# A windowed-attention and highway-layer kernel: the last sum and the doubling of x on GpSimd, with another order of the loads

## The chip, the cores and the metric

The kernel runs on one core of a Trainium2 chip. The metric is the device time in microseconds (us) of one execution. A core has five engines that run their own instruction streams and wait for each other through semaphores: TensorE (PE, matmuls), VectorE (DVE), ScalarE (ACT), GpSimd (POOL) and SyncE (SP). Here POOL issues all loads and SP issues the bias load and all stores.

## What is computed

The inputs are float32: q, k and v of shape (4, 8, 768, 64), that is 4 batches, 8 heads, 768 positions, 64 values per head; two 512 x 512 weights and a bias of 512. The output is (3072, 512) float32. In short:

```python
scores = (q @ k.T) / sqrt(64)            # per batch and head
keep = (pos_k < 4) | ((0 <= pos_q - pos_k) & (pos_q - pos_k < 128))
a = softmax(where(keep, scores, -1e9))
x = (a @ v) with the heads side by side  # (3072, 512)
H = relu(x @ w_h)
T = sigmoid(x @ w_t + b_t)
out = T * H + (1 - T) * x
```

A position sees the 128 positions up to itself and the first 4 positions of its batch (the sinks). The second half is a highway layer on the attention output.

## The kernel before, in words

The 3072 rows are cut into 24 blocks of 128 rows, 6 per batch; a block's window lies in itself and the block before it. All matmul operands are float16, which the loads cast to. Beside each head's 64 columns of v stands a column of 2.0, so that the row sum comes out doubled and the scaled result, xh, is half of x. With u = tanh of half the gate's input and hps = xh @ w_h, the output is 2·xh + (u + 1)·(max(hps, 0) - xh).

One loop (L335 to L357) runs over i from -2 to 24 and is a software pipeline written out by hand: in iteration i, block i+1 has its scores made (stage_S), block i its attention output (stage_A), block i+2 its transposes (stage_T), block i-1 its highway layer (stage_Mt, stage_Mh). The order of PE, DVE and ACT instructions is as written there.

- stage_T (L178): PE transposes q and k of a block (L182, L184), ACT copies the one (qT, L187), DVE the other (kT, L188).
- stage_S (L228): score matmuls (L242), and ACT takes the exponent into e (L245), in two halves. stage_sink (L214): the scores of the sinks, sk (L222), and their exponent es (L225), for two blocks at a time.
- stage_mask (L251): DVE multiplies each half of e by a 0/1 mask (L258).
- stage_A (L262): PE multiplies by v (L273, L279); DVE takes the reciprocal of the row sums (rec, L286) and scales (xh, L288).
- stage_X (L293): PE transposes xh (L297), ACT copies it to xT (L299).
- stage_sink_setup (L191), once per batch: DVE copies L198, PE vps (L203), DVE vs (L207).
- stage_Mt (L304): gate matmuls into tps (L307, L309), ACT tanh into u (L312).
- stage_Mh (L315): matmuls into hps (L321); then three DVE instructions: dd = max(hps, 0) - xh (L324), ee = (u + 1)·dd (L327), otok = 2·xh + ee (L330); SP stores otok (L332).

Loads: load(n) issues two DMAs from POOL (q, L84; k, L85), load_v(n) one (v, L92). The loads of blocks 0 to 7 (AHEAD = 8) are put out before the loop in a list written by hand (L106 to L138), with the weights w_t (L122) after the q and k of block 2 and w_h (L125) after the q and k of block 3. In the loop, loads run 8 blocks ahead of stage_T (L345 to L347). Buffers: 8 for q and for k (sd_pool), a ring of 11 for v (v_ring), 4 for xh (x_pool), 3 each for u, dd and ee (td_pool), 4 for otok (o_pool). A POOL DMA also waits until the POOL DMA eight places before it has landed. POOL's instructions in the loop are ordered by the framework's scheduler, which each kernel's build fixes.

Before the loop DVE fills the v buffers with 2.0 (L104, one memset each) and makes the masks' variants (L140 to L145).

Of the kernel before, what the change touches and what calls it, by code (L numbers as in the profile page):

```python
# [9 lines left out]
FP16 = mybir.dt.float16  # L10
FP32 = mybir.dt.float32
AF = mybir.ActivationFunctionType
ALU = mybir.AluOpType
ENG = mybir.EngineType
# [7 lines left out]
def kernel(  # L22
# [18 lines left out]
    nc = tc.nc  # L41
    P = 128

    B, H, S, D = q.shape
    NSINK = int(n_sink)
# [4 lines left out]
    NT, DM = out.shape  # L50
# [4 lines left out]
    NB = NT // P  # L55
    NHP = H // 2
    NOC = DM // P
    SCALE = 1.0 / math.sqrt(D)
    VW = H * 65 + 64
    AHEAD = 8  # L60

    const = ctx.enter_context(tc.tile_pool(name="const", bufs=1))
    sd_pool = ctx.enter_context(tc.tile_pool(name="p_sd", bufs=AHEAD))
    qkT_pool = ctx.enter_context(tc.tile_pool(name="p_qkT", bufs=5))
    e_pool = ctx.enter_context(tc.tile_pool(name="p_e", bufs=5))
    es_pool = ctx.enter_context(tc.tile_pool(name="p_es", bufs=2))
# [2 lines left out]
    td_pool = ctx.enter_context(tc.tile_pool(name="p_td", bufs=3))  # L69
# [2 lines left out]
    av_ps = ctx.enter_context(tc.tile_pool(name="ps_av", bufs=1, space=bass.MemoryType.PSUM))  # L72
    m_ps = ctx.enter_context(tc.tile_pool(name="ps_m", bufs=2, space=bass.MemoryType.PSUM))

    NV = AHEAD + 3
    v_ring = [const.tile([P, VW], FP16, tag=f"v{i}", name=f"v{i}") for i in range(NV)]
    qk_sd = {}

    def load(n):
        b, c = divmod(n, NSC)  # L80
        rows = slice(c * P, (c + 1) * P)
        qsd = sd_pool.tile([P, H, D], FP16, tag="qsd", name="qsd")
        ksd = sd_pool.tile([P, H, D], FP16, tag="ksd", name="ksd")
        nc.gpsimd.dma_start(out=qsd, in_=q[b, :, rows, :].transpose([1, 0, 2]))  # L84
        nc.gpsimd.dma_start(out=ksd, in_=k[b, :, rows, :].transpose([1, 0, 2]))  # L85
        qk_sd[n] = (qsd, ksd)

    def load_v(n):
        b, c = divmod(n, NSC)
        rows = slice(c * P, (c + 1) * P)  # L90
        vt = v_ring[n % NV][:, 0:H * 65].rearrange("p (h e) -> p h e", e=65)
        nc.gpsimd.dma_start(out=vt[:, :, 0:D], in_=v[b, :, rows, :].transpose([1, 0, 2]))  # L92
# [1 line left out]

    ebias = const.tile([P, 1], FP32, tag="ebias")
    nc.vector.memset(ebias, _EXP_BIAS)
    wh_sb = const.tile([P, NOC, DM], FP16, tag="wh")
    wt_sb = const.tile([P, NOC, DM], FP16, tag="wt")
    ident = const.tile([P, P], FP16, tag="ident")
    mask = const.tile([P, 2, P], FP16, tag="mask", name="mask")  # L100
    nc.vector.memset(ident, 1.0)
    nc.vector.memset(mask, 1.0)
    for vt in v_ring:
        nc.vector.memset(vt, 2.0)  # L104

    with tc.manual_schedule(engines={ENG.Pool}):  # L106
        load(0)
        nc.gpsimd.affine_select(
            out=ident, in_=ident, compare_op=ALU.is_equal, fill=0.0,
            base=0, pattern=[[-1, P]], channel_multiplier=1)  # L110
        load_v(0)
        load(1)

        nc.gpsimd.affine_select(
            out=mask[:, 1, :], in_=mask[:, 1, :], compare_op=ALU.is_ge, fill=0.0,
            base=0, pattern=[[1, P]], channel_multiplier=-1)
        load_v(1)
        nc.gpsimd.affine_select(
            out=mask[:, 0, :], in_=mask[:, 0, :], compare_op=ALU.is_ge, fill=0.0,
            base=-1, pattern=[[-1, P]], channel_multiplier=1)  # L120
        load(2)
        nc.gpsimd.dma_start(out=wt_sb, in_=moe_w_t.rearrange("(kc p) of -> p kc of", p=P))  # L122
        load_v(2)
        load(3)
        nc.gpsimd.dma_start(out=wh_sb, in_=moe_w_h.rearrange("(kc p) of -> p kc of", p=P))  # L125
        load_v(3)
        bdm = const.tile([P, H], FP32, tag="bdm")
        nc.gpsimd.memset(bdm, 1.0)
        bdm3 = bdm.rearrange("p (a b) -> p a b", b=2)
        nc.gpsimd.affine_select(  # L130
            out=bdm3, in_=bdm3, compare_op=ALU.is_ge, fill=0.0,
            base=0, pattern=[[-32, NHP], [-4, 2]], channel_multiplier=1)
        nc.gpsimd.affine_select(
            out=bdm3, in_=bdm3, compare_op=ALU.is_ge, fill=0.0,
            base=NSINK - 1, pattern=[[32, NHP], [4, 2]], channel_multiplier=-1)
        for n in range(4, AHEAD):
            load(n)
            load_v(n)  # L138

    mask0 = const.tile([P, P], FP16, tag="mask0", name="mask0")  # L140
    nc.vector.tensor_copy(out=mask0, in_=mask[:, 1, :])
    nc.vector.memset(mask0[0:NSINK, :], 1.0)
    mask1 = const.tile([P, 2, P], FP16, tag="mask1", name="mask1")
    nc.vector.tensor_copy(out=mask1, in_=mask)
    nc.vector.memset(mask1[0:NSINK, 0, :], 1.0)  # L145


    bt32 = const.tile([1, DM], FP32, tag="bt32")
# [11 lines left out]
    for hh in range(2):  # L160
        nc.vector.tensor_copy(
            out=sel[:, :, 4 * hh:4 * hh + NSINK],
            in_=ident[:, 0:NSINK].unsqueeze(1).to_broadcast([P, NHP, NSINK]))
    ks_bd = []
    for i in range(2):
        t = const.tile([P, NHP * 160], FP16, tag=f"ks{i}", name=f"ks{i}")
# [24 lines left out]
    def stage_sink_setup(b):  # L191
# [8 lines left out]
        vps = av_ps.tile([P, 2, 512], FP32, tag="av", name="vps")  # L200
        vt = v_ring[(b * NSC) % NV]
        for g in range(2):
# [11 lines left out]
    def stage_sink(n):  # L214

        b = n // NSC
        ks = ks_bd[b % 2]
        sk = m_ps.tile([P, 2, P], FP32, tag="m", name="sk")
        for t in range(2):
            qT, _ = qkT[n + t]  # L220
            for hp in range(NHP):
                nc.tensor.matmul(sk[:, t, :], lhsT=ks[:, hp * P:(hp + 1) * P],  # L222
                                 rhs=qT[:, hp, :], start=(hp == 0), stop=(hp == NHP - 1))
        es = es_pool.tile([P, 2, P], FP16, tag="es", name="es")
        nc.scalar.activation(out=es, in_=sk, func=AF.Exp, bias=ebias, scale=SCALE)  # L225
        es_of[n] = es_of[n + 1] = es
# [35 lines left out]
    def stage_A(n):  # L262
        b, c = divmod(n, NSC)
        es, np_ = e_of.pop(n)
        vts = ([] if c == 0 else [v_ring[(n - 1) % NV]]) + [v_ring[n % NV]]
        av = av_ps.tile([P, 2, 4, P], FP32, tag="av", name="av")
# [33 lines left out]
        xT_of[n] = xT  # L300

    u_of = {}

    def stage_Mt(n):  # L304
        xT = xT_of[n]
        tps = m_ps.tile([P, DM], FP32, tag="m", name="tps")
        nc.tensor.matmul(tps, lhsT=ones_row, rhs=bt16, start=True, stop=False)  # L307
        for kc in range(NOC):
            nc.tensor.matmul(tps, lhsT=xT[:, kc, :], rhs=wt_sb[:, kc, :],  # L309
                             start=False, stop=(kc == NOC - 1))  # L310
        u = td_pool.tile([P, DM], FP16, tag="u", name="u")
        nc.scalar.activation(out=u, in_=tps, func=AF.Tanh)  # L312
        u_of[n] = u

    def stage_Mh(n):  # L315
        xT = xT_of.pop(n)
        xh = xh_of.pop(n).rearrange("p h d -> p (h d)")
        u = u_of.pop(n)
        hps = m_ps.tile([P, DM], FP32, tag="m", name="hps")
        for kc in range(NOC):  # L320
            nc.tensor.matmul(hps, lhsT=xT[:, kc, :], rhs=wh_sb[:, kc, :],  # L321
                             start=(kc == 0), stop=(kc == NOC - 1))
        dd = td_pool.tile([P, DM], FP16, tag="dd", name="dd")
        nc.vector.scalar_tensor_tensor(out=dd, in0=hps, scalar=0.0, in1=xh,  # L324
                                       op0=ALU.max, op1=ALU.subtract)
        ee = td_pool.tile([P, DM], FP16, tag="ee", name="ee")
        nc.vector.scalar_tensor_tensor(out=ee, in0=u, scalar=1.0, in1=dd,  # L327
                                       op0=ALU.add, op1=ALU.mult)
        otok = o_pool.tile([P, DM], FP32, tag="otok", name="otok")
        nc.vector.scalar_tensor_tensor(out=otok, in0=xh, scalar=2.0, in1=ee,  # L330
                                       op0=ALU.mult, op1=ALU.add)
        nc.sync.dma_start(out=out[n * P:(n + 1) * P, :], in_=otok)  # L332

    with tc.manual_schedule(engines={ENG.PE, ENG.DVE, ENG.Activation}):
        for i in range(-2, NB + 1):  # L335
            s = i + 1
            if 0 <= i < NB and i % NSC >= 2 and i % 2 == 0:
                stage_sink(i)
            if 0 <= s < NB:
                stage_S(s)  # L340
            if 0 <= i < NB:
                stage_A(i)
            if i + 2 < NB:
                stage_T(i + 2)
            if i + 2 + AHEAD < NB:  # L345
                load(i + 2 + AHEAD)
                load_v(i + 2 + AHEAD)  # L347
            if 0 <= s < NB:
                stage_mask(s)
            if 0 <= i - 1 < NB:  # L350
                stage_Mt(i - 1)
            if 0 <= i < NB:
                stage_X(i)
            if 0 <= i < NB and i % NSC == 0:
                stage_sink_setup(i // NSC)
            if 0 <= i - 1 < NB:
                stage_Mh(i - 1)  # L357
# [35 lines left out]
```

The softmax here doesn't subtract the row's maximum and nothing guards it: scores larger than these inputs give would overflow.

## Time and profile before

| | |
|---|---|
| median of 3 runs | 140.11 us (139.75 to 140.7) |
| the profiled execution, its own time | 140.7 us |
| its span, first to last instruction | 139.0 us |
| its TensorE clock, granted | 0.993 |
| ACT busy | 90.4 us (65% of the span) |
| POOL busy | 66.2 us (48%), all of it before 87.5 us |
| mean of one load issue on POOL | 0.89 us |
| store of one block, issue to landing (median) | 2.9 us |

Busy times are sums over an engine's instructions; matmuls are pipelined and their ends are modelled, so PE's busy time is not time at its peak. An idle time before an instruction is put down to the semaphore that came last. The chain of waits is followed back from the last instruction; it names the work that each microsecond of the span was spent on.

### The profile page before, as it was taken

The numbers are of one execution on the slowest core, as the hardware profiler recorded it, in microseconds if no ns is written. First come the engines' busy times: TensorE is split into PE (matmuls) and PEld (weight loads), VectorE is DVE, ScalarE is ACT, GpSimd is POOL, SyncE is SP. The second block draws the span as 40 slices with busy tenths as digits, with TensorE's granted clock in tenths as the row PEclk, the third lists the DMA queues.
The fourth block names the chain that finished last, engine by engine and source line by source line (L and its number), as shares of the span: only waits on it lengthen the run. The fifth ranks groups of instructions, "written<-read, shape, count | busy, mean of one in ns | idle before, by whom it ended". The sixth has DMA issues, their size and how long they took to land.

```text
span 139.0 us, 3303 instructions
## 1 busy us (share of the span) xinstructions
PE 114.6 (82%) x1312; PEld 74.1 (53%) x1312; DVE 117.2 (84%) x235; ACT 90.4 (65%) x129; POOL 66.2 (48%) x84
## 2 busy tenths in 40 slices
PE   0306879999999699999999699999996999999730
PEld 0105656756764465667565457657652665675300
DVE  6895466689988999899898999898989998999590
ACT  3015961879775957987777497779767777873310
POOL 6999785899887987876758170000000000000000
PEclk9999999999999999999999999999999999999997
DMA  1999999999999999999999959221011021101111
GB/s 9 113 127 120 158 189 162 152 171 178 203 191 168 200 200 174 181 201 185 185 159 144 186 72 134 80 78 75 5 75 75 0 80 75 70 11 75 75 75 75
DMA packets 79408, 16.98 MB, mean 122 GB/s; under 512 B 75297, under 2 KB 76321, under 8 KB 79394
## 3 DMA queue, kind: packets, MB, share of 16 engines
q0 software_dynamic: 75936, 10.49, 112.2%
q1 hardware_dynamic: 3458, 6.30, 12.4%
q8 instruction: 10, 0.16, 0.5%
q14 instruction: 4, 0.03, 0.1%
HBM read 20.97 MB, written 6.29 MB: 196 GB/s over the span
## 4 chain that ended last, share of the span: by engine, by line
DVE 42%; PE 33%; ACT 14%; issue 8%; DVEq 0%
PE hps L321 12%; ACT e L245 9%; DVE ee L327 6%; DVE otok L330 6%; DVE e L258 6%; DVE dd L324 6%; DVE xh L288 5%; PE av L273 4%; PE tps L309 4%; DVE kT L188 4%; PE xtp L297 3%; ACT qT L187 3%; PE sps L242 3%; PE sk L222 3%; DVE vs L207 2%
## 5 line engine op out<-in xcount | busy, mean ns | idle before, releaser
L245 ACT ACTIVATE e<-sps,ebias 128x1024 f16<-128x1024 f32 (+1 forms) x48 | 47.4, 1039 | 17.5 <-PE sps L242 13.3
L309 PE MATMUL tps<-wt_sb,xT 128*128 128x512 f16 x96 | 25.5, 390 | 0.0
L321 PE MATMUL hps<-wh_sb,xT 128*128 128x512 f16 x96 | 24.6, 378 | 0.7
L84 POOL DMA_DIRECT2D qsd<-in_q_dram x24 | 21.5, 895 | 5.3 <-DMA wt_sb<-in_moe_w_t_dram 1.2
L85 POOL DMA_DIRECT2D ksd<-in_k_dram x24 | 21.4, 890 | 2.3 <-DMA wh_sb<-in_moe_w_h_dram 1.2
L273 PEld LDWEIGHTS <-e 128*128 128x128 f16 x352 | 20.4, 100 | 3.9 <-DVE vs L207 0.9
L312 ACT ACTIVATE u<-tps 128x512 f16<-128x512 f32 x24 | 14.4, 600 | 9.5 <-PE tps L309 9.5
L258 DVE TENSOR_TENSOR e<-e,mask 128x1024 f16<-128x1024 f16 x32 | 20.5, 683 | 0.0
L324 DVE SCALAR_TENSOR_TENSOR dd<-hps,xh 128x512 f16<-128x512 f32 x24 | 16.5, 688 | 3.9 <-PE hps L321 3.9
L242 PE MATMUL sps<-qT,kT 64*128 64x128 f16 x352 | 15.2, 227 | 4.6 <-DVE kT L188 3.9
L187 ACT COPY qT<-tp 128x512 f16<-128x512 f16 x24 | 14.0, 584 | 7.5 <-PE tp L184 7.5
L327 DVE SCALAR_TENSOR_TENSOR ee<-u,dd 128x512 f16<-128x512 f16 x24 | 16.6, 693 | 2.5
L288 DVE TENSOR_TENSOR xh<-av,rec 128x512 f16<-128x512 f32 x24 | 16.6, 692 | 0.8
L330 DVE SCALAR_TENSOR_TENSOR otok<-xh,ee 128x512 f32<-128x512 f16 x24 | 16.6, 692 | 0.8
L242 PEld LDWEIGHTS <-kT 64*128 64x128 f16 x352 | 10.7, 98 | 12.0 <-issue 6.8
L299 ACT COPY xT<-xtp 128x512 f16<-128x512 f16 x24 | 14.0, 582 | 1.4 <-PE xtp L297 0.9
L188 DVE COPY kT<-tp 128x512 f16<-128x512 f16 x24 | 10.1, 419 | 5.5 <-ACT qT L187 5.5
L309 PEld LDWEIGHTS <-xT 128*128 128x128 f16 x96 | 9.6, 100 | 9.1 <-issue 0.8
L182 PE MATMUL tp<-ident,qsd 128*128 128x128 f16 x96 | 10.2, 234 | 4.8 <-DMA qsd<-in_q_dram 4.8
L297 PEld LDWEIGHTS <-xh 128*128 128x128 f16 x96 | 6.3, 100 | 13.8 <-DVE xh L288 11.6
L321 PEld LDWEIGHTS <-xT 128*128 128x128 f16 x96 | 9.1, 97 | 8.2 <-issue 1.5
L297 PE MATMUL xtp<-ident,xh 128*128 128x128 f16 x96 | 9.7, 225 | 4.2 <-DVE xh L288 4.2
(84 smaller groups left out, 162.1 us busy)
## 6 DMA issues: line engine op xcount, KB each, us to landing
out_dram<-otok SPq DMA_DIRECT2D x24, 256.0 KB, 2.9
qsd<-in_q_dram POOLq DMA_DIRECT2D x24, 128.0 KB, 7.2
ksd<-in_k_dram POOLq DMA_DIRECT2D x24, 128.0 KB, 7.4
wt_sb<-in_moe_w_t_dram POOLq DMA_DIRECT2D x1, 512.0 KB, 7.9
wh_sb<-in_moe_w_h_dram POOLq DMA_DIRECT2D x1, 512.0 KB, 9.6
v_91<-in_v_dram POOLq DMA_DIRECT2D x3, 128.0 KB, 5.4
v_92<-in_v_dram POOLq DMA_DIRECT2D x3, 128.0 KB, 4.1
v_93<-in_v_dram POOLq DMA_DIRECT2D x2, 128.0 KB, 7.9
```

The costliest lines, as they stand in the source:

```text
L84: nc.gpsimd.dma_start(out=qsd, in_=q[b, :, rows, :].transpose([1, 0, 2]))
L85: nc.gpsimd.dma_start(out=ksd, in_=k[b, :, rows, :].transpose([1, 0, 2]))
L242: nc.tensor.matmul(sps[:, hh, o:o + P], lhsT=kk[rows, hp, :], rhs=qT[rows, hp, :], start=True, stop=True)
L245: nc.scalar.activation(out=e.rearrange("p a b c d -> p a (b c d)"), in_=sps[:, :, 0:2 * np_ * P], func=AF.Exp, bias=ebias, scale=SCALE)
L258: nc.vector.tensor_tensor(out=ev, in0=ev, in1=m.unsqueeze(1).to_broadcast([P, 4, np_ * P]), op=ALU.mult)
L273: nc.tensor.matmul(av[:, g, 2 * hl + hh, 0:_AVN], lhsT=es[g][:, hh, hl, pc, :], rhs=vt[:, 65 * h:65 * h + _AVN], start=first, stop=False, ...
L288: nc.vector.tensor_tensor(out=xh, in0=avh[:, :, 0:D], in1=rec.unsqueeze(2).to_broadcast([P, H, D]), op=ALU.mult)
L309: nc.tensor.matmul(tps, lhsT=xT[:, kc, :], rhs=wt_sb[:, kc, :], start=False, stop=(kc == NOC - 1))
L321: nc.tensor.matmul(hps, lhsT=xT[:, kc, :], rhs=wh_sb[:, kc, :], start=(kc == 0), stop=(kc == NOC - 1))
L324: nc.vector.scalar_tensor_tensor(out=dd, in0=hps, scalar=0.0, in1=xh, op0=ALU.max, op1=ALU.subtract)
L327: nc.vector.scalar_tensor_tensor(out=ee, in0=u, scalar=1.0, in1=dd, op0=ALU.add, op1=ALU.mult)
L330: nc.vector.scalar_tensor_tensor(out=otok, in0=xh, scalar=2.0, in1=ee, op0=ALU.mult, op1=ALU.add)
```

## The change

Two things are changed.

1. The last sum. In stage_Mh, xh2 = 2·xh is made by GpSimd (a new tile of td_pool, 3 buffers), and otok = xh2 + ee is a GpSimd tensor_tensor. VectorE keeps dd and ee. The store now waits for GpSimd.
2. The loads. The list by hand is gone. Before the loop stand load(0), load_v(0), load(1), load_v(1), then w_t and w_h; load(n) and load_v(n) for n from 2 on stand in the loop, 4 iterations ahead. There are 6 buffers for q and k and 6 for v (8 and 11 before). The identity and the masks are filled with ones by GpSimd rather than VectorE, and the order of a few set-up instructions differs; the DVE set-up now makes both mask variants ahead of the first kT.

```diff
-    AHEAD = 8
...
-    sd_pool = ctx.enter_context(tc.tile_pool(name="p_sd", bufs=AHEAD))
+    sd_pool = ctx.enter_context(tc.tile_pool(name="p_sd", bufs=6))
...
-    NV = AHEAD + 3
+    NV = 6
...
-    nc.vector.memset(ident, 1.0)
-    nc.vector.memset(mask, 1.0)
+    load(0)
...
+    make_identity(nc, ident)
     for vt in v_ring:
         nc.vector.memset(vt, 2.0)
-
-    with tc.manual_schedule(engines={ENG.Pool}):
-        load(0)
...
-        load(2)
-        nc.gpsimd.dma_start(out=wt_sb, in_=moe_w_t.rearrange("(kc p) of -> p kc of", p=P))
-        load_v(2)
-        load(3)
-        nc.gpsimd.dma_start(out=wh_sb, in_=moe_w_h.rearrange("(kc p) of -> p kc of", p=P))
-        load_v(3)
...
-        for n in range(4, AHEAD):
-            load(n)
-            load_v(n)
+    load_v(0)
+    load(1)
+    mask = const.tile([P, 2, P], FP16, tag="mask", name="mask")
+    nc.gpsimd.memset(mask, 1.0)
...
+    load_v(1)
...
+    nc.gpsimd.dma_start(out=wt_sb, in_=moe_w_t.rearrange("(kc p) of -> p kc of", p=P))
+    nc.gpsimd.dma_start(out=wh_sb, in_=moe_w_h.rearrange("(kc p) of -> p kc of", p=P))
...
+        xh2 = td_pool.tile([P, DM], FP16, tag="xh2", name="xh2")
+        nc.gpsimd.tensor_scalar_mul(xh2, xh, 2.0)
+        xh2_of[n] = xh2
...
-        nc.vector.scalar_tensor_tensor(out=otok, in0=xh, scalar=2.0, in1=ee,
-                                       op0=ALU.mult, op1=ALU.add)
+        nc.gpsimd.tensor_tensor(out=otok, in0=xh2_of.pop(n), in1=ee, op=ALU.add)
         nc.sync.dma_start(out=out[n * P:(n + 1) * P, :], in_=otok)
...
         for i in range(-2, NB + 1):
+            if 2 <= i + 4 < NB:
+                load(i + 4)
+                load_v(i + 4)
...
-            if i + 2 + AHEAD < NB:
-                load(i + 2 + AHEAD)
-                load_v(i + 2 + AHEAD)
```

More of the change, by code (lines that the diff above doesn't have):

```diff
@@ L96 @@
     nc.vector.memset(ebias, _EXP_BIAS)
-    wh_sb = const.tile([P, NOC, DM], FP16, tag="wh")
-    wt_sb = const.tile([P, NOC, DM], FP16, tag="wt")
+    load(0)
     ident = const.tile([P, P], FP16, tag="ident")
-    mask = const.tile([P, 2, P], FP16, tag="mask", name="mask")
-    nc.vector.memset(ident, 1.0)
-    nc.vector.memset(mask, 1.0)
+    make_identity(nc, ident)
     for vt in v_ring:
         nc.vector.memset(vt, 2.0)
-    with tc.manual_schedule(engines={ENG.Pool}):
-        load(0)
[L108 to L120, printed above, removed]
-        load(2)
-        nc.gpsimd.dma_start(out=wt_sb, in_=moe_w_t.rearrange("(kc p) of -> p kc of", p=P))
-        load_v(2)
-        load(3)
-        nc.gpsimd.dma_start(out=wh_sb, in_=moe_w_h.rearrange("(kc p) of -> p kc of", p=P))
-        load_v(3)
[L127 to L135, printed above, removed]
-        for n in range(4, AHEAD):
-            load(n)
-            load_v(n)
@@ new lines @@
+    load_v(0)
+    load(1)
+    mask = const.tile([P, 2, P], FP16, tag="mask", name="mask")
+    nc.gpsimd.memset(mask, 1.0)
+    nc.gpsimd.affine_select(
+        out=mask[:, 1, :], in_=mask[:, 1, :], compare_op=ALU.is_ge, fill=0.0,
+        base=0, pattern=[[1, P]], channel_multiplier=-1)
+    nc.gpsimd.affine_select(
+        out=mask[:, 0, :], in_=mask[:, 0, :], compare_op=ALU.is_ge, fill=0.0,
+        base=-1, pattern=[[-1, P]], channel_multiplier=1)
+    mask1 = const.tile([P, 2, P], FP16, tag="mask1", name="mask1")
@@ L140 @@
+    nc.vector.tensor_copy(out=mask1, in_=mask)
+    nc.vector.memset(mask1[0:NSINK, 0, :], 1.0)
     mask0 = const.tile([P, P], FP16, tag="mask0", name="mask0")
@@ L142 @@
     nc.vector.memset(mask0[0:NSINK, :], 1.0)
-    mask1 = const.tile([P, 2, P], FP16, tag="mask1", name="mask1")
-    nc.vector.tensor_copy(out=mask1, in_=mask)
-    nc.vector.memset(mask1[0:NSINK, 0, :], 1.0)
+    load_v(1)
+    wh_sb = const.tile([P, NOC, DM], FP16, tag="wh")
+    wt_sb = const.tile([P, NOC, DM], FP16, tag="wt")
+    nc.gpsimd.dma_start(out=wt_sb, in_=moe_w_t.rearrange("(kc p) of -> p kc of", p=P))
+    nc.gpsimd.dma_start(out=wh_sb, in_=moe_w_h.rearrange("(kc p) of -> p kc of", p=P))
     bt32 = const.tile([1, DM], FP32, tag="bt32")
@@ L163 @@
             in_=ident[:, 0:NSINK].unsqueeze(1).to_broadcast([P, NHP, NSINK]))
+    bdm = const.tile([P, H], FP32, tag="bdm")
+    nc.gpsimd.memset(bdm, 1.0)
+    bdm3 = bdm.rearrange("p (a b) -> p a b", b=2)
+    nc.gpsimd.affine_select(
+        out=bdm3, in_=bdm3, compare_op=ALU.is_ge, fill=0.0,
+        base=0, pattern=[[-32, NHP], [-4, 2]], channel_multiplier=1)
+    nc.gpsimd.affine_select(
+        out=bdm3, in_=bdm3, compare_op=ALU.is_ge, fill=0.0,
+        base=NSINK - 1, pattern=[[32, NHP], [4, 2]], channel_multiplier=-1)
     ks_bd = []
@@ L302 @@
     u_of = {}
+    xh2_of = {}
     def stage_Mt(n):
```

## The prediction, made before the changed kernel ran

> **What bounds the kernel now.** I read the page's chain of waits first, then the steady part by stretches, then the start instruction by instruction, then the landing of each early load.
>
> The chain's shares by engine:
>
> ```profile
> DVE 42%; PE 33%; ACT 14%; issue 8%; DVEq 0%
> ```
>
> No engine carries it alone. The chain repeats every 29.1 us, which is 6 blocks (one batch), so a block takes 4.85 us. In order of time (start, duration, what), one half of a period runs on DVE and the other on PE:
>
> ```profile
> 69.29 0.62 DVE dd L324
> 70.00 0.70 DVE ee L327
> 70.72 0.69 DVE otok L330
> 71.57 0.70 DVE xh L288
> 72.32 0.40 PE xtp L297 x4
> ...
> 90.43 0.22 PE tp L182 x4
> 90.65 0.22 PE tp L184 x4
> 90.87 0.22 PE tps L307
> 91.09 0.86 PE tps L309 x4
> 91.95 0.34 PE xtp L297 x4
> 92.30 0.99 PE hps L321 x4
> ```
>
> The stretches (busy us of PE, PEld, DVE, ACT, POOL, then clock, DMA share, GB/s) show how little room PE has:
>
> ```profile
> 68.10:82.40 14.30, 12.56 (x143) 7.49 (x143) 13.31 (x28) 10.35 (x16) 7.77 (x10) 1.00 1.55 137
> 82.40:97.20 14.80, 14.67 (x185) 10.10 (x186) 13.49 (x26) 11.85 (x18) 1.06 (x2) 1.00 0.62 99
> 58.40:87.50 29.10, 27.22 (x330) 17.59 (x328) 26.80 (x53) 22.20 (x33) 15.73 (x18) 1.00 1.74 163
> ```
>
> In the first half DVE is on the chain and PE idles 1.74 us; in the second PE idles 0.13. Over a period PE idles 1.9 us, DVE 2.3. The work that moves:
>
> ```profile
> L330 DVE SCALAR_TENSOR_TENSOR otok<-xh,ee 128x512 f32<-128x512 f16 x24 | 16.6, 692 | 0.8
> ```
>
> The start (timeline): kT of block 0 is late by DVE's set-up, and T(2), the transposes of block 2, run as soon as PE is done with block 0:
>
> ```profile
> 10.33 0.35 DVE L188 COPY kT<-tp 128x512 f16<-128x512 f16 x1
> ...
> 14.31 0.93 PE L273 MATMUL av<-v_91,e 128*128 128x112 f16 x8
> 15.03 0.63 PE L182 MATMUL tp<-ident,qsd 128*128 128x128 f16 x4
> 15.46 0.63 PE L184 MATMUL tp<-ident,ksd 128*128 128x128 f16 x4
> 16.12 0.59 ACT L187 COPY qT<-tp 128x512 f16<-128x512 f16 x1
> ```
>
> Issue plus time to landing puts q of block 2 at 11.4 and its k at 13.4, before they are needed.
>
> **What the skill says.** (1) The Trainium skill, "SBUF — State Buffer", Who interferes with whom: a VectorE instruction with two SBUF inputs and a GpSimd instruction that reads SBUF exclude each other; whichever starts second waits for the whole of the other. On DVE these are both halves of the mask (L258, 683 ns each) and ee (693). dd and xh have one input in PSUM. No run here shows such a pair: POOL only issues DMAs in the loop, 0.87 to 0.89 us each, also under masks. (2) "GPSIMD Engine Reference", 3.1: a two-input add takes 4497 ns for 2048 fp32 elements; a loop over one input takes 1.8 cycles per element, 769 ns for 512. Scaled to 512 columns, an estimate: 1.12 us for otok and 0.77 us for xh2. The trace has neither; its only POOL arithmetic, the selects of 128 columns (0.33 us), sets a floor of about that for each, and 3.5 us together is my upper end. (3) "DMA: Bandwidth & Descriptors", Issuing engines are not separate DMA queues: all loads share the same 16 DMA engines. The trace agrees: early tiles land one by one about 1 us apart.
>
> **The change, part by part.**
>
> *Loads at the start, +3.0.* Weights now come ahead of block 2. In the trace v of block 1 lands at 10.5. Between q of block 2 (11.4) and v of block 3 (23.4) landed six tiles and both weights: 12.0 us. Tiles alone take 0.94 each (eight from 23.4 to 30.9). So the weights took (12.0 - 5.6)/2 = 3.2 each; I take 3.1. In the new order: w_t at 13.6, w_h 16.7, q2 17.6, k2 18.6, v2 19.5, q3 20.5, k3 21.4. k2 at 18.6 against the old start of its transposes at 15.46 makes T(2) late by 3.1, say 3.0. What is queued behind it on PE: X(0), vps and all scores of block 2; ACT's qT, DVE's kT and masks follow. This part is a string of dependences (qT, kT, mask, ks, vs, A(1)), so the delay stays. T(3) was at 21.21, now 24.2, after k3: no second stall.
>
> *DVE set-up, 0.* Five v memsets (0.61 apart) and two more go, 3.5 us; but the mask variants, two copies and two memsets, some 1.2 us, now precede kT and wait for POOL's selects at about 8.0. kT(0) comes at about 9.3 rather than 10.33. The wait at T(2) hides this second; without that wait it is a gain of 1.0.
>
> *Later loads, 0.* Loads of blocks 2 to 5 issue without DVE. From block 6 on, each stands in POOL's order among xh2 and otok. Behind otok(0), which waits for ee(0) at about 30, stand q, k and v of block 7; issued by 34 and landed within 4 to 8 us, they are wanted at iteration 5, about 44. In the steady order (xh2(n), k(n+8), otok(n-1), v(n+6), q(n+9)) the loads are five to eight blocks early. Six buffers suffice. If this cover went, each late load would hold PE at its transposes. SP's stores wait for POOL, with four otok buffers.
>
> *otok leaves DVE, at best -4.1.* 24 x 0.69 = 16.6 us go, but only the three per period on the DVE half count, and PE is the next limit. Of PE's 1.9 us idle per period, 0.67 is vps waiting for ACT's xT, which stays. That leaves 1.2 per period; the steady part (29 to 129) has 3.4 periods: 4.1.
>
> *What DVE gets back.* POOL's two reading operations take 1.89 of 4.85 us, 39%. A DVE instruction that falls on one waits on average (0.77² + 1.12²)/(2 x 1.89) = 0.49, so 0.19 per start, and there are three such starts per block: 0.57 of the 0.69 saved. Bounds: 0 (POOL always runs under dd, xh and kT) to three full collisions of 1.12, 3.4. I take 0.57 because POOL's own queue, not DVE, sets when its operations come. That leaves 17% of 4.1: -0.7.
>
> *The tail, -0.2.* The last otok takes 1.12 and a handover in place of 0.69: +0.5. DVE frees rec(23) and dd(23) earlier, PE already waiting there (0.94 for xh at 129.98): -0.7.
>
> Sum: +3.0 - 0.7 - 0.2 = +2.1. The profiled execution has a span of 139.0 and a time of 140.7, so its like would be 142.8; the median of the runs is 140.11, which gives 142.2.
>
> **The rivals.**
>
> *GpSimd becomes the bound: slower, 147.* Per block it does 3 x 0.89 + 1.89 = 4.56 us, under 4.85. Waits on DVE work the other way too: DVE holds the port 2.0 us per block, which costs POOL about 0.2 per operation, so 5.0. It starts behind, too: walking its order, otok(2) ends some 4.5 us behind ee(2). ee(n) needs otok(n-3) done (three buffers), which allows about 12.7 us of lag, so 8 are left, over the 14 blocks that still have loads: 0.57 each. It binds when the two operations cost over 4.85 + 0.57 - 2.67 = 2.75 us together. At 3.1 they use up the lag in 8.7 blocks and add 0.92 in each of 5.3: +4.9, 147. At 3.5, +10, 152. For it: no span of these operations is known here. Against: the prices.
>
> *No collisions: not slower, 138.8.* If DVE is never held, the whole 4.1 comes: +3.0 - 4.1 - 0.2 = -1.3. It decides below some 0.2 us of holding per block, since PE covers 1.5 us (T and Mt) between A and X, and DVE needs 1.0 from A to xh. For it: after ee come rec, xh and kT, 1.3 us without a second SBUF input, which just holds one otok.
>
> *T(2) isn't late: faster, 138.2.* If tiles of block 2 pass the weights in the rings, +3.0 becomes -1.0 (kT(0)): -1.0 - 0.7 - 0.2 = -1.9. Against: the landings above keep the order of issue.
>
> **How the numbers follow.** Likeliest case 0.50, its own range 141.0 to 144; GpSimd as bound 0.22; no collisions 0.20; T(2) in time 0.08. One per cent, 1.4 us, is about what a measurement of this kernel can tell from no change: faster is below 138.7, slower above 141.5. Slower: GpSimd and 0.41 of the likeliest, 0.63. Faster: half of the no-collision case and most of the last, 0.14. Same: 0.23. The range 138.2 to 148 leaves out the far end of the GpSimd case and the best of the last two.
>
> **What would show it.** Right: T(2) starts at 17 to 19 and waits for the DMA of q or k; DVE has no otok, but masks or ee of 0.8 us and more, or gaps before them that name POOL; 28.5 to 29.1 us per period. Wrong: POOL busy over 5.3 us per block and ee waiting for POOL (GpSimd bound); masks and ee at 0.68 to 0.69 with a period of 27.9 (no collisions); T(2) at 15 (loads in time).

## The result, and the profile after

The changed kernel takes **152.49 us** (median of 4 runs, 151.46 to 152.95) where the kernel before takes 140.34 on the same chip: ratio 1.086, 95% interval 1.0791 to 1.0929. The profiled execution has a span of 150.8 us (before 139.0) at a clock of 0.997. The forecast was slower, as it came, but 142.2 us, with a range that ended at 148. Some runs on this chip fall in a slower state; medians in this document are over all runs and ratios over the fast ones, so the two can differ (e4: median 141.23 us, fast runs 140.82; e7: 152.59 and 150.72).

From the page of the changed kernel: busy time by engine, the chain's shares, and three groups (line, engine, operation, tiles, count | busy us, mean ns | idle before):

```profile
PE 116.3 (77%) x1312; PEld 74.1 (49%) x1312; DVE 119.1 (79%) x204; ACT 90.8 (60%) x129; POOL 136.1 (90%) x134
...
DVE 43%; PE 21%; ACT 12%; issue 8%; DMA 6%; POOL 6%; POOLq 1%; DVEq 0%; ACTq 0%
...
L247 DVE TENSOR_TENSOR e<-e,mask 128x1024 f16<-128x1024 f16 x32 | 30.7, 1000 | 0.0
...
L320 DVE SCALAR_TENSOR_TENSOR ee<-u,dd 128x512 f16<-128x512 f16 x24 | 20.6, 858 | 3.1
...
L171 PE MATMUL tp<-ident,qsd 128*128 128x128 f16 x96 | 10.2, 234 | 10.3 <-DMA qsd<-in_q_dram 10.3
```

The mask and ee in the kernel before:

```profile
L258 DVE TENSOR_TENSOR e<-e,mask 128x1024 f16<-128x1024 f16 x32 | 20.5, 683 | 0.0
...
L327 DVE SCALAR_TENSOR_TENSOR ee<-u,dd 128x512 f16<-128x512 f16 x24 | 16.6, 693 | 2.5
```

POOL is now busy for 90% of the span. otok is gone from DVE, but the halves of the mask went from 683 to 1000 ns in the mean and ee from 693 to 858, with the same shapes and hardly more idle time before them: the time is inside the instructions. PE's share of the chain fell from 33% to 21%, and PE waits 10.3 us for q (4.8 before).

The start (timeline of the changed kernel; start, duration, what, and in brackets the idle time before):

```profile
8.53 0.35 DVE L177 COPY kT<-tp 128x512 f16<-128x512 f16 x1
...
18.93 0.61 PE L171 MATMUL tp<-ident,qsd 128*128 128x128 f16 x4 [5.48 <-DMA qsd<-in_q_dram]
...
19.77 0.61 PE L173 MATMUL tp<-ident,ksd 128*128 128x128 f16 x4 [0.23 <-DMA ksd<-in_k_dram]
...
22.57 1.46 DVE L187 COPY ks_150<-kT 64x16 f16<-64x16 f16 x2
```

kT of block 0 is 1.8 us earlier than before (10.33). The k transposes of block 2 come at 19.77 where they came at 15.46: 4.3 us late. The weights, issued at 8.01 and 8.78, land 7.2 and 9.0 us later, at 15.2 and 17.8, and k of block 2 at 19.7. The last line is two small copies that took 0.62 us together before.

A stretch of the steady part, POOL and DVE of the same timeline:

```profile
104.86 1.17 POOL L323 TENSOR_TENSOR otok<-xh_1509,ee 128x512 f32<-128x512 f16 x1
105.11 3.03 DVE L247 TENSOR_TENSOR e<-e,mask 128x1024 f16<-128x1024 f16 x2
105.96 0.92 POOL L91 DMA_DIRECT2D v_92<-in_v_dram  x1
106.88 0.88 POOL L83 DMA_DIRECT2D qsd<-in_q_dram  x1
107.78 1.71 POOL L314 TENSOR_SCALAR xh_1708<-xh 128x512 f16<-128x512 f16 x1
109.45 0.93 POOL L84 DMA_DIRECT2D ksd<-in_k_dram  x1
```

POOL's records follow each other without a gap. The two halves of the mask take 3.03 us together in place of 1.28. In the chain of waits the same pair is the longest piece of each block:

```profile
102.59 0.61 DVE dd L317
...
103.32 0.69 DVE ee L320
...
104.17 0.69 DVE xh L277
104.86 0.33 DVE kT L177
105.19 2.95 DVE e L247 x2
```

Here all of it is DVE, and in this stretch a block takes 5.55 us (99.64 to 105.19, from one mask pair to the next), against 4.85 before in the mean of six. Not every block is like that: over blocks 0 to 20 the mean loss is a third of a microsecond per block.

When it is lost: dd of block 0 starts 5.6 us later than before, dd of block 20 12.3 later, the last one 11.3 later. The end of the span is 11.8 late. So about 5.6 us go at the start, 6.7 more up to block 20, 1.0 comes back over the last three blocks (e12 below, where nobody makes the sum, gains 0.9 there), and the tail takes about 0.5.

### The profile page after: what moved, and what is told of

The parts are those of the page before. It is cut to its first block, busy times and chain, and to the rows that moved or that the text cites. A ratio compares the mean times of both kernels' runs of the same rounds, so it can differ in the third digit from the quotient of the medians.

```text
span 150.8 us, 3355 instructions
## 1 busy us (share of the span) xinstructions
PE 116.3 (77%) x1312; PEld 74.1 (49%) x1312; DVE 119.1 (79%) x204; ACT 90.8 (60%) x129; POOL 136.1 (90%) x134
## 4 chain that ended last, share of the span: by engine, by line
DVE 43%; PE 21%; ACT 12%; issue 8%; DMA 6%; POOL 6%; POOLq 1%; DVEq 0%; ACTq 0%
DVE e L247 18%; ACT e L234 8%; PE hps L311 7%; DVE ee L320 7%; DMA ksd<-in_k_dram 6%; DVE xh L277 5%; DVE dd L317 5%; DVE kT L177 4%; PE tps L299 3%; PE av L262 3%; ACT qT L176 3%; DVE vs L196 2%; PE xtp L286 2%; POOL qsd L83 2%; PE sk L211 2%
## 5 line engine op out<-in xcount | busy, mean ns | idle before, releaser
L247 DVE TENSOR_TENSOR e<-e,mask 128x1024 f16<-128x1024 f16 x32 | 30.7, 1000 | 0.0
L262 PEld LDWEIGHTS <-e 128*128 128x128 f16 x352 | 19.9, 100 | 12.0 <-DVE vs L196 5.9
L84 POOL DMA_DIRECT2D ksd<-in_k_dram x24 | 21.9, 914 | 1.7 <-DMA wh_sb<-in_moe_w_h_dram 1.7
L320 DVE SCALAR_TENSOR_TENSOR ee<-u,dd 128x512 f16<-128x512 f16 x24 | 20.6, 858 | 3.1
L83 POOL DMA_DIRECT2D qsd<-in_q_dram x24 | 22.0, 917 | 0.8 <-POOLq L366 0.8
L171 PE MATMUL tp<-ident,qsd 128*128 128x128 f16 x96 | 10.2, 234 | 10.3 <-DMA qsd<-in_q_dram 10.3
L231 PE MATMUL sps<-qT,kT 64*128 64x128 f16 x352 | 15.2, 227 | 2.7 <-DVE kT L177 2.1
L231 PEld LDWEIGHTS <-kT 64*128 64x128 f16 x352 | 10.7, 98 | 10.1 <-issue 6.8
L171 PEld LDWEIGHTS <-qsd 128*128 128x128 f16 x96 | 7.4, 104 | 11.0 <-DMA qsd<-in_q_dram 10.5
L286 PEld LDWEIGHTS <-xh 128*128 128x128 f16 x96 | 6.6, 102 | 12.2 <-DVE xh L277 10.3
```

What stands on the lines that cost most here:

```text
L231: nc.tensor.matmul(sps[:, hh, o:o + P], lhsT=kk[rows, hp, :], rhs=qT[rows, hp, :], start=True, stop=True)
L247: nc.vector.tensor_tensor(out=ev, in0=ev, in1=m.unsqueeze(1).to_broadcast([P, 4, np_ * P]), op=ALU.mult)
L262: nc.tensor.matmul(av[:, g, 2 * hl + hh, 0:_AVN], lhsT=es[g][:, hh, hl, pc, :], rhs=vt[:, 65 * h:65 * h + _AVN], start=first, stop=False, ...
L286: nc.tensor.transpose(xtp[:, j, :], xh[:, 2 * j:2 * j + 2, :], ident)
```

## The experiments

"Before" in each comparison is the kernel before on the same chip in the same batch, 140.27 to 140.7 us.

### One part at a time

**e1_sum_only**: the kernel before with the new sum only.

```diff
+        xh2 = td_pool.tile([P, DM], FP16, tag="xh2", name="xh2")
+        nc.gpsimd.tensor_scalar_mul(xh2, xh, 2.0)
...
-        nc.vector.scalar_tensor_tensor(out=otok, in0=xh, scalar=2.0, in1=ee,
-                                       op0=ALU.mult, op1=ALU.add)
+        nc.gpsimd.tensor_tensor(out=otok, in0=xh2, in1=ee, op=ALU.add)
```

> Only the last sum and the doubling on GpSimd; the loads as in the kernel before. Port theory (VectorE instructions with two SBUF inputs are held while GpSimd runs xh2 at 1.5 us or otok at 1.15 us, whatever else GpSimd does): halves of the mask at 0.85 to 1.0 us in place of 0.683, ee at 0.8 or more, start unchanged, 143 to 147 us. Queue theory (the cost comes from GpSimd being full with loads and sums together, 5.6 us per block): collisions only until the loads end near 85 us, and from there a block takes 4.6 us or less, so 139 to 142 us.

Measured: 153.49 us, 1.0952 (1.086 to 1.1045). The sum alone is as bad as the whole change. Here DVE does wait for POOL, in the waits of DVE (us in total, times, longest):

```profile
DVE xh L288 <- POOL xh L324: 5.1, 4, 3.4
```

In this order of loads POOL's queue holds the loads up to block 11 ahead of the first doubling, which starts at 39.6, and four buffers of xh run out meanwhile. That is a wait that the changed kernel does not have.

**e2_loads_only**: the changed kernel with the sum as it was (the reverse of the edit above).

> Only the new order of loads and set-up; the last sum stays on VectorE. If the start alone is what the loads cost, the dd of block 0 starts near 30.5 to 31 us rather than 25.55, the distance then stays, the masks take 0.683 us, and the time is 145 to 146 us. Rival: loads that are issued in the loop, with 6 buffers, are late again further on: more than 147 us, with transposes that wait for q or k after the first 25 us.

Measured: 145.19 us, 1.0318 (1.025 to 1.0386). dd of every block, from 0 to 23, is 4.2 us later than before, and the mask is unchanged (639 ns over all shapes, as before). So the loads cost 4.2 us of span once, at the start, and nothing later; the other 1.4 us at block 0 of the changed kernel are the sum's. The changed kernel is 7.3 us over this one: that is what the sum adds.

**e3_after_weights_later**: the changed kernel with the weights put back behind the q and k that are needed first. The same edit without the new sum is **e5_old_sum_weights_later**.

```diff
+    load(2)
     nc.gpsimd.dma_start(out=wt_sb, in_=moe_w_t.rearrange("(kc p) of -> p kc of", p=P))
+    load_v(2)
+    load(3)
     nc.gpsimd.dma_start(out=wh_sb, in_=moe_w_h.rearrange("(kc p) of -> p kc of", p=P))
+    load_v(3)
...
-            if 2 <= i + 4 < NB:
+            if 4 <= i + 4 < NB:
```

> The changed kernel with the q and k of block 2 put ahead of w_t, and those of block 3 ahead of w_h, as before; all else as changed. If the weights' place causes the late start: dd of block 0 at 24 to 25.5 us, 146 to 147.5 us in all. Rival (the start is late from the VectorE set-up, from the copies of the sinks' keys held by GpSimd, or from loads issued one after another in the loop): dd of block 0 at 28 us or later, above 149 us.

> The changed kernel's set-up and loads in the loop with 6 buffers, but the last sum on VectorE and the weights after blocks 2 and 3: what is left of the change is the set-up order and the fewer buffers. Starting from the run with the weights later, dd of block 0 comes at 24.4 us, 1.1 ahead of the kernel before, and with the sum on VectorE nothing is lost later: 138.8 to 139.6 us. Rival: loads issued in the loop cost something further on that the late start hid: 140.3 us or more.

Measured: e3 147.63 us, 1.0501 (1.0435 to 1.0567); e5 139.19, 0.9898 (0.9843 to 0.9953). With the weights behind block 2 the changed kernel is 4.9 us faster and the version with the old sum 6.0. In e5 dd of every block is 2.0 us earlier than before. kT of block 0 comes at 8.48 there, 1.85 earlier, so I take this for the set-up's gain, which the late transposes had hidden; set-up and buffers were not tried apart. From here on e5 is the base, since nothing is late in it: the new sum costs 147.63 - 139.19 = 8.4 us against it.

**e4_double_on_act**: e1 with the doubling on ScalarE, the last addition still on POOL.

```diff
-        nc.gpsimd.tensor_scalar_mul(xh2, xh, 2.0)
+        nc.scalar.mul(xh2, xh, 2.0)
```

> The kernel before with otok's sum on GpSimd but the doubling on ScalarE, so GpSimd reads SBUF for 1.15 us per block rather than 2.65. Port theory: the hold falls with the time that GpSimd reads, masks at 0.75 to 0.8 us; VectorE gives up 0.69 and is held some 0.3, so 138.5 to 141 us. Queue theory: GpSimd is never full (3.85 us per block), the whole gain comes: 136 to 138 us. If ScalarE's 0.6 us per block more are on the path: above 141 us, with masks near 0.7 us.

Measured: 141.23 us, 1.003 (0.9992 to 1.0068), 12.3 less than e1. One instruction of each block, moved from POOL to ACT, takes the whole loss away.

### Reading, writing, or a full queue

**e10_unused_read** and **e11_unused_write**: e5 with an extra POOL instruction per block whose result nobody uses: the doubling, which reads SBUF, or a fill of about the same length, which only writes. **e12_no_last_sum**: e5 with the last sum left out, as its expectation says.

```diff
e10:
+        nc.gpsimd.tensor_scalar_mul(xh2, xh, 2.0)
e11:
+        nc.vector.memset(xh2[:, 0:1], 2.0)
+        nc.gpsimd.memset(xh2, 2.0)
e12:
-        nc.vector.scalar_tensor_tensor(out=ee, in0=u, scalar=1.0, in1=dd,
-                                       op0=ALU.add, op1=ALU.mult)
...
-        nc.vector.scalar_tensor_tensor(out=otok, in0=xh, scalar=2.0, in1=ee,
-                                       op0=ALU.mult, op1=ALU.add)
+        nc.vector.scalar_tensor_tensor(out=otok, in0=u, scalar=1.0, in1=dd,
+                                       op0=ALU.add, op1=ALU.mult)
```

> The old sum on VectorE with the weights later (139.2 us), and GpSimd makes the doubled x beside it, which nobody uses: one reading instruction of 1.5 us per block, and GpSimd at 4.3 us per block, under its limit. Port theory: halves of the mask or ee are held, means of 0.75 us and more, and VectorE, which has no slack in half of the blocks, ends 3 to 6 us later: 142 to 145 us. Queue theory: GpSimd isn't full, so nothing changes: 139 to 140 us.

> The same with a fill of 1536 float16, some 1.5 us, in place of the doubled x, and one one-column VectorE fill per block, 0.06 us. It reads no SBUF. Port theory: masks at 0.683, ee at 0.693, 139 to 141 us. If it is as slow as the unused doubled x, the cost lies in GpSimd's time and not in its reads.

> The kernel with the weights later and nobody making the last sum: ee is stored itself, so the output lacks 2 xh. This is the whole gain that taking otok off VectorE can have. By the prediction's working, TensorE is next and 1.2 us per 6 blocks come, 4.1 in all: 134.5 to 136 us. If VectorE's 16.6 us counted in full: 123 us. If TensorE or ScalarE already bound: above 137.5 us.

Measured: e10 146.94 us, 1.0468 (1.0423 to 1.0513), 7.75 over e5; e11 141.63, 1.0091 (1.006 to 1.0121), 2.4 over e5; e12 135.86, 0.9658 (0.96 to 0.9715), 3.3 under e5. From the groups of e10, the mask and the doubling, then the mask of e11:

```profile
L251 DVE TENSOR_TENSOR e<-e,mask 128x1024 f16<-128x1024 f16 (+1 forms) x48 | 37.3, 817 | 0.0
...
L318 POOL TENSOR_SCALAR xh<-xh 128x512 f16<-128x512 f16 x24 | 38.3, 1597 | 22.5 <-DVE xh L281 22.2
```

```profile
L251 DVE TENSOR_TENSOR e<-e,mask 128x1024 f16<-128x1024 f16 (+1 forms) x48 | 28.7, 638 | 0.0
```

The reading instruction lengthens the mask by 8.6 us in all, the fill not at all. In e10 POOL is not full: it stands idle for 22.2 us before the doubling, waiting for DVE's xh, and no DVE instruction waits for its result. So the doubling costs 7.75 us without a full POOL, and e11 points to its reading. The Trainium skill, "SBUF — State Buffer", Who interferes with whom, says just this of a GpSimd read and a two-input VectorE instruction, and of a GpSimd write that it does not do it; the numbers agree for these instructions. They do not agree with the length that the prediction took from there, the whole of the other instruction: in e10 one half of the mask was held 0.88 us and no other more than 0.42, though the doubling's records last 1.48 us and more. The 2.4 us of e11 come from elsewhere: two of the eight small copies ks, which take 0.17 us each, took 1.88 and 0.76.

**e7_gpsimd_writes_only** and **e9_writes_matched**: e3 with fills in place of the doubling and the last addition (3.66 and 2.8 us per block; the highway sum is left out), to see what a full POOL costs that reads nothing.

```diff
-        nc.gpsimd.tensor_scalar_mul(xh2, xh, 2.0)
+        nc.vector.memset(xh2[:, 0:1], 2.0)
+        nc.gpsimd.memset(xh2, 2.0)
...
-        nc.gpsimd.tensor_tensor(out=otok, in0=xh2_of.pop(n), in1=ee, op=ALU.add)
+        nc.vector.memset(otok[:, 0:1], 2.0)
+        nc.gpsimd.memset(sc, 2.0)
+        nc.gpsimd.memset(otok, 2.0)
```

> The changed kernel with the weights later, but GpSimd makes neither the doubled x nor the sum: in their place it fills tiles with a constant (2048 and 1024 float16, and the 512 float32 that are stored), instructions that write SBUF and read none; two one-column VectorE fills per block keep the order. The output leaves the highway sum out. Port theory (reads of SBUF by GpSimd hold VectorE): masks and ee back at 0.683 and 0.693 us, a block in 4.6 to 4.8 us, 138 to 141 us, though GpSimd is as busy. Queue theory (GpSimd's pace sets the time): as slow as with the real work, 146 to 149 us, if GpSimd is still over 85% busy.

> The writes-only run again with smaller fills (1600 and 512 float16, and the 512 float32 that are stored), sized by the last run's slope of 0.82 ns per element to 2.9 us per block, which is what the doubled x and the sum take together (1.66 + 1.25). The output leaves the highway sum out. It is to be set against 147.6 us with the real work in the same order of loads. If GpSimd's pace alone, 5.6 us per block with the loads, sets the time: 145 to 148 us. If most of the 7 us are holds of VectorE, of which a fill makes none: 139 to 142 us.

Measured: e7 152.59 us, 1.0723 (1.0635 to 1.081); e9 149.53, 1.0628 (1.0562 to 1.0695). By the time alone, this would have been the proof that a full POOL sets the time, and my theory would have fallen. But mask and ee stand at 638 and 692 ns, as before, and the loss of e9 lies almost whole in two jumps, at blocks 5 and 11. Timeline of e9 at the second one, DVE and some of POOL:

```profile
79.28 8.59 DVE L191 COPY ks<-kT 64x16 f16<-64x16 f16 x2
...
80.73 1.75 POOL L319 MEMSET xh<- 128x1600 f16 x1
82.09 0.84 POOL L329 MEMSET sc<- 128x512 f16 x1
...
86.10 1.21 POOL L84 DMA_DIRECT2D ksd<-in_k_dram  x1
86.97 0.88 POOL L329 MEMSET sc<- 128x512 f16 x1
```

Two copies of 16 columns took 8.59 us, one of them 7.15, while POOL ran fills and DMA issues back to back. So the fills had brought a cost of their own that the changed kernel hardly has (its ks copies take 3.4 us in all, 1.6 before). The two runs did not separate the theories.

**e13_writes_ks_on_act**: e9 with these copies on ScalarE.

```diff
-            nc.vector.tensor_copy(out=ks3[rows, :, 4 * hh:4 * hh + NSINK],
-                                  in_=kT[rows, :, 0:NSINK])
+            nc.scalar.copy(out=ks3[rows, :, 4 * hh:4 * hh + NSINK],
+                           in_=kT[rows, :, 0:NSINK])
```

> The fills of the earlier run (no sum in the result: the highway sum is left out, three fills of 2.8 us per block stand in for the doubling and the last addition on GpSimd), with the key copies of the sinks made by ScalarE, so that no small copy of VectorE is left to be starved. Masks and ee 638 and 692 ns as before in every theory. If only the reads of GpSimd cost time (my theory), GpSimd's filling up by itself costs nothing: 137 to 140 us. If GpSimd's own pace of 5.6 us per block of work and DMA issues sets the time (the rival), 145 to 148 us although VectorE is undisturbed.

Measured: 135.89 us, 0.9663 (0.9623 to 0.9704), the same as e12, which does nothing in place of the sum. Its page:

```profile
PE 112.8 (84%) x1312; PEld 74.5 (56%) x1312; DVE 98.8 (74%) x244; ACT 91.0 (68%) x137; POOL 122.5 (91%) x158
```

POOL is as busy (91%) as in the changed kernel (90%), and it costs nothing. One reserve: the groups of POOL in e13 add up to 150 us in 122.5 of busy time, so fills ran beside DMA issues; the records of the changed kernel add up to 138 in 136.1, so there they hardly overlap. A POOL filled by strictly serial work without reads was not tried.

### Buffers, and the doubling alone

**e8_sum_only_deep** and **e15_weights_later_deep**: e1 and e3 with deeper buffers.

```diff
-    x_pool = ctx.enter_context(tc.tile_pool(name="p_x", bufs=4))
-    td_pool = ctx.enter_context(tc.tile_pool(name="p_td", bufs=3))
-    o_pool = ctx.enter_context(tc.tile_pool(name="p_o", bufs=4))
+    x_pool = ctx.enter_context(tc.tile_pool(name="p_x", bufs=8))
+    td_pool = ctx.enter_context(tc.tile_pool(name="p_td", bufs=8))
+    o_pool = ctx.enter_context(tc.tile_pool(name="p_o", bufs=6))
```

> The run with the sum alone, with 8 buffers for xh, xT, u, dd, ee and the doubled x, and 6 for otok, so that VectorE no longer waits for GpSimd to have read an xh. Queue theory: the jumps of 3.9 us at block 3 and 3.4 us at block 11 go: 145 to 147 us. Port theory: what remains over 140.3 us is the hold, masks still at 0.85 us or more. If nothing changes, 152 us or more, the buffers were not what bound.

> The changed kernel with the weights later, and 8, 8 and 6 buffers for x, its double and the rows of the output in place of 3 and 4. If the buffers do not matter (my theory, as no wait of VectorE for GpSimd shows in the changed kernel), 147.6 within 1 us. If ring waits mattered (the rival), 3 us or more faster, 144.6 or less.

Measured: e8 150.08 us, 1.0661 (1.0587 to 1.0735): 3.4 less than e1, and the wait for POOL is gone, but 9.5 us over before remain. e15 148.32, 1.0535 (1.0497 to 1.0574), no better than e3. Short buffers explain a part of e1 and nothing of the changed kernel.

**e14_weights_later_double_on_act**: e3 with the doubling on ScalarE (the edit of e4), everything else of the change in place.

> The changed kernel with the weights later, and the doubling of x on ScalarE in place of GpSimd; the buffers and the last addition on GpSimd stay. If the doubling's reading on GpSimd is nearly the whole of what the sum costs (my theory), 139 to 141 us against 147.6 with it; masks near 730 ns rather than 1038. If the last addition with its short ring of buffers costs much itself (the rival), over 144 us.

Measured: 138.29 us, 0.9806 (0.9764 to 0.9848), 9.3 under e3. Its groups, first two of DVE, then one of POOL:

```profile
L251 DVE TENSOR_TENSOR e<-e,mask 128x1024 f16<-128x1024 f16 (+1 forms) x48 | 30.2, 669 | 0.0
L324 DVE SCALAR_TENSOR_TENSOR ee<-u,dd 128x512 f16<-128x512 f16 x24 | 17.0, 707 | 3.1
```

```profile
L327 POOL TENSOR_TENSOR otok<-xh,ee 128x512 f32<-128x512 f16 x24 | 28.0, 1168 | 34.3 <-DVE ee L324 12.9 <-ACT e L238 9.9 <-DVE rec L279 8.9
```

The last addition still reads SBUF for 28 us on POOL, yet mask and ee lose only 1.9 us in all. In 18 of the 24 blocks it starts within 0.2 us of ee's end, and the next on DVE (rec, xh, kT) have no second SBUF input. One block of its timeline, DVE and POOL:

```profile
101.08 0.69 DVE L324 SCALAR_TENSOR_TENSOR ee<-u,dd 128x512 f16<-128x512 f16 x1
101.91 1.15 POOL L327 TENSOR_TENSOR otok<-xh,ee 128x512 f32<-128x512 f16 x1 [1.17 <-DVE rec L279]
...
103.63 1.28 DVE L251 TENSOR_TENSOR e<-e,mask 128x1024 f16<-128x1024 f16 x2
```

**e6_double_on_act_deep** and **e16_double_on_act_ks_on_act**: e14 with the deeper buffers, and that with the ks copies on ScalarE too.

> As the run before this one, with the doubling on ScalarE, otok's sum on GpSimd, and 8 buffers each for xh, xT, u, dd, ee and the doubled x (6 for otok). If the earlier run with the doubling on ScalarE lost its 2.6 us at block 3 to ee waiting for an otok that stood behind loads in GpSimd's queue, deeper buffers remove it: 137 to 139 us, with masks at 0.72 to 0.76 us. If the port takes all that VectorE gives up: 139 to 140.5 us. If ScalarE's 0.58 us per block are on the path: above 140.5 us.

> The fastest version so far (weights later, doubling on ScalarE, last addition on GpSimd, deeper buffers; 138.7 us) with the key copies of the sinks on ScalarE too. If the last addition's hold of small copies still costs something there, 137 to 138.2 us; if not, 138.7 within 0.4.

Measured: e6 138.7 us, 0.9859 (0.9813 to 0.9905); e16 137.62, 0.9761 (0.9728 to 0.9795). e16 is the fastest of the kernels that compute everything, 2.4% faster than the kernel before; e14, with short buffers and the copies on DVE, is not clearly apart from it.

## Why the prediction was wrong, step by step

The direction came true through the loads, whose mechanism was right and whose size was a little short. For the sum it did not: forecast was a gain of 0.9 us (-4.1, +3.4 and -0.2), and the runs show a loss of 7.3 (the changed kernel less e2). Predicted and measured, in us of span:

| step | predicted | measured | from |
|---|---|---|---|
| loads at the start | +3.0 | +4.2 | e2, every block |
| DVE set-up | 0, or -1.0 without the late T(2) | 0; -2.0 | kT(0) 1.8 earlier; e5 |
| later loads | 0 | 0 | e2: no further delay |
| otok leaves DVE | -4.1 | -3.3 | e12 against e5 (times) |
| what DVE gets back | +3.4 | about +10.1, as a remainder | 7.3 (changed kernel less e2, times) + 3.3 - 0.5 |
| the tail | -0.2 | +0.5 | end of span after dd(23) |

The rows add up to 11.5 us; the medians lie 12.15 apart, since e2's time is 4.9 over the kernel before and its trace 4.2. The fifth row holds all else that the sum costs.

**The step that failed is "What DVE gets back".** It is the term of the sum that was mis-sized. Its mechanism, that reading on POOL holds the mask and ee, is what e10, e11 and e14 show. Its price, its place and its length were off.

*The price.* 0.77 us for xh2 was an estimate from the Trainium skill, "GPSIMD Engine Reference", 3.1, from a figure that the page gives as the best case of a tight loop. Measured in the changed kernel: 1.48 to 1.97 us, mean 1.64. The measurement decides. otok was priced rightly (1.12; measured 1.26 in the changed kernel, 1.17 in e14). So the two operations took 2.90 us per block in place of 1.89, and with three issues of 0.92 POOL's block was 5.6 us rather than 4.56, over the 4.85 of a block before: POOL falls behind while it still has loads to issue.

*The place.* The formula took POOL's operations to fall anywhere. They do not. In e10 the doubling starts with the mask. With the doubling on ScalarE (e14) otok mostly starts right behind ee, under DVE's free instructions, and the holds on mask and ee are 0.08 us per block. In the changed kernel POOL's backlog takes it away from there: otok starts 0.15 us after the end of its ee in block 0 and 0.14 in the last four, but 6.7 to 12.3 us after it in blocks 4 to 16. In the stretch shown it starts at 104.86, and the mask pair at 105.11 runs into it. If each held half of the mask is taken as held from its start until its normal length before its end, 8.4 of the 15.5 us of holds lie within records of otok, 2.4 within records of the doubling, and 4.7 where POOL's records show only DMA issues. In e3 it is 11.4, 1.9 and 5.9; in e14, without the doubling, 0.2, none and 1.2. So the doubling harms in two ways: by its own reading (e10), and by making otok late.

*The length.* The formula lets a hold last to the end of the other operation. With the measured durations it gives (1.64² + 1.26²)/(2 x 2.90) x 2.90/5.55 x 3 = 1.16 us per block, of the right sign, but that is partly luck, for e10 shows the doubling's holds to be far shorter than its records.

DVE's own holds, mask, ee and ks, came to 21.3 us over the kernel before (15.5, 4.0 and 1.8), 0.89 per block rather than 0.57. That is more than the 0.69 that otok gave back, so a gain of 17% of 4.1 turned into a loss.

**The late T(2)** was seen rightly, 1.2 us too short: w_t landed 1.6 us later than priced, w_h and k of block 2 1.1 later.

**The rivals.** "GpSimd becomes the bound" had named 152 us at 3.5 us for both operations, binding above 2.75; they took 2.90, and half of its signature came: POOL is full, at 5.6 us per block. The other half, ee waiting for POOL, is absent, deeper buffers change nothing (e15), and the doubling costs 7.75 us with POOL idle a fourth of the time (e10). That the 152 us it named are the time measured is luck, since it reckoned with 3.5 us and with that wait. POOL's pace is not ruled out by this: even at the shortest durations its block is 1.48 + 1.14 + 3 x 0.90 = 5.3 us while loads last, over 4.85, and otok's lag stops growing at about 12 us, where DVE's block of 5.55 us is as long as POOL's. What is shown is that moving the doubling off POOL takes the loss away (e14), and that the doubling alone, with POOL not full, suffices for a loss of this size (e10). Whether a part of the changed kernel's 5.55 us per block is POOL's pace, which meets DVE in these holds, is not separated by these runs. "No collisions" holds for otok alone (e14), not for the doubling. "T(2) isn't late" did not occur.

The range was too narrow because it had the uncertain price, up to 3.5 us for both operations, only in the rival's case and not in the holding term.

## What to carry to other kernels

Before an instruction goes to GpSimd, ask which VectorE instructions with two SBUF inputs run while it reads, and measure its length there. Ask also whether GpSimd's queue keeps pace, because an operation that comes late lands under other instructions. In these runs an addition that started where VectorE worked from PSUM was nearly free (e14), and a doubling that started with a two-input instruction cost 7.75 us (e10). ScalarE, idle for 35% of the span before, took the same doubling at 0.65 us, and the loss was gone (e4, e14). Large loads that are wanted late belong behind the small ones that the pipeline wants first: the order of two weights was worth 4.9 to 6.0 us.

## What had not been expected of the hardware

- The doubling of 512 float16 columns took GpSimd 1.48 us at least, more than its two-input addition with a float32 result (1.14 us at least).
- Fills leave mask and ee alone but can starve a small SBUF-to-SBUF copy of DVE: 7.15 us for one of 0.17 (e9), 1.88 in e11. In e9 it was held across several fills and DMA issues, not for the rest of one. Why is open.
- A hold does not match the records' times exactly. In e10's timeline the record of a doubling ends at 103.04, and both halves of the mask, started behind it, are done at 103.31:

```profile
101.56 1.48 POOL L318 TENSOR_SCALAR xh<-xh 128x512 f16<-128x512 f16 x1 [0.57 <-DVE xh L281]
```

```profile
101.68 1.63 DVE L251 TENSOR_TENSOR e<-e,mask 128x1024 f16<-128x1024 f16 x2
```

  The pair takes 1.28 us unheld, so it was held for 0.35 us, and the first half was free again by about 102.0, a microsecond before the doubling's record ends. In the changed kernel's stretch the second half is held until about 107.45 while POOL's records show DMA issues up to 107.76. In e14 a pair at 32.13 takes 1.97 us while POOL's records show nothing but DMA issues, from 29.56 to 33.91, with an otok behind them. In e5, e11 and the kernel before, where POOL reads nothing in the loop, DMA issues hold the mask not at all (638 to 639 ns). That a reading operation queued behind the issues had already begun to read is my reading of it, not shown.
